# FFN2's seven products in another order, and three small moves around them, in a one-core mLSTM + FFN kernel

## The chip, the core and the metric

The kernel runs on one core of a Trainium2 chip. The core has engines with a queue each, which run side by side and meet only through semaphores: PE (TensorE, matrix products, with PEld for its weight loads), DVE (VectorE), ACT (ScalarE), POOL (GpSimd) and SP (SyncE, which here only issues DMAs). PE writes its products into PSUM, eight banks per partition; DVE and ACT read them from there. The metric is the time of one execution in microseconds (us) on the device; lower is better.

## The reference

An mLSTM cell over 4 batches, 8 heads, 768 steps and 40 features per head, and behind it a feed-forward network with a squared ReLU. The cell's output, 3072 rows of 320 features, is the network's input.

```python
for t in range(S):                       # per batch and head
    m_new = maximum(f[t] + m, i[t])
    fs, is_ = exp(f[t] + m - m_new), exp(i[t] - m_new); m = m_new
    C = fs * C + is_ * outer(v[t], k[t]);  n = fs * n + is_ * k[t]
    y[t] = sigmoid(o[t]) * (C @ q[t]) / maximum(abs(n @ q[t]), 1)
x = y.transpose(0, 2, 1, 3).reshape(3072, 320)
h = maximum(x @ w_in, 0)                 # 320 -> 2048
out = (h * h) @ w_out                    # 2048 -> 320
```

The FFN weights come as 8-byte floats, which the kernel rounds early on; these products are fp32.

## The kernel before

**Tiling.** The sequence is cut into 24 blocks of 128 tokens (`s` = 0..23, six for each batch), and the FFN into 12 groups of two blocks, 256 tokens (`g` = 0..11). Attention of block `s` is computed chunk-wise: scores, weighted values, a carried state C, and the numerators, which DVE turns (`tn`, L858) and SP stores to DRAM (`store_num`, L873) and loads back token by token (`load_num`, L878). `normalise_turned` (L883 to L903, DVE) then makes the FFN's input rows x, which go through DRAM once more (`store_rows` L931, `load_rows` L936) and are turned by DVE into `xT` (L943).

**FFN2 as seven products.** The second FFN product of groups 1 to 11 (`ffn2_fast`, L1066) takes the 256 tokens x 2048 hidden x 320 outputs as 2 x 2 blocks and needs seven block products in place of eight. Call the blocks of the hidden values A11, A12, A21, A22 (first index: token half; second: even or odd hidden blocks) and those of w_out B11 to B22. Sums of weight blocks (T0, T1, T2, and B12 overwritten by a difference) are made once. Sums of the A blocks are made by DVE for each group in `sums` (L1044 to L1056), 128 x 1024 elements each: S1 = A21 + A22, S2 = S1 - A11, then "S3" = A11 - A21, which overwrites A21, and S4 = A12 - S2. A product (`product`, L1058 to L1061) is 8 fp32 matmuls of 128 x 160 that accumulate in one bank; the trace records 16 instructions for it.

The seven products, in PE's order, with the bank and the reader of each:

| | product | bank | read by |
|---|---|---|---|
| 1 | A11 B11 | X | ACT copies it to m1 (L1081) |
| 2 | S2 T1 | Y | DVE: u12 = Y + m1 (L1077) |
| 3 | A12 B21 | on top of X | ACT copies it to the output y0 (L1086) |
| 4 | S3 B12 | on top of Y | DVE: m1 += Y |
| 5 | S1 T0 | X' | DVE: u22 = m1 + X' |
| 6 | A22 T2 | Y' | DVE: m1 += Y' |
| 7 | S4 B22 | on top of X' | DVE: u12 += X' |

All five DVE additions have the line L1077. `ffn2_fast` is called in four steps: step 0 issues products 1 and 2, step 1 products 3 and 4, step 2 products 5 and 6, step 3 product 7.

**The order of the work.** The kernel runs under a manual schedule: each engine executes its instructions in the order in which the program issues them, and the tile layer adds the semaphore waits (a reader waits for the writer, and a writer of a bank or tile waits for the last reader of what it overwrites). The main loop (L1440 on) walks through `parts`: for each `g` four steps of FFN2 of group `g` and four parts of FFN1 of group `g + 2` (`ffn1_open` L1145, `ffn1_close` L1178, `ffn1_rows` L1161). Each run of four parts carries one attention block: even `s` goes with FFN2, odd `s` with FFN1. A block for which `joined(s)` holds (even, 10 or later) has its first half of attention inside the FFN1 part before. Five PSUM banks (`ps_h`) serve FFN1, FFN2 and half of the scores; three (`ps_at`) the rest of attention. A new `ps_h` tile gets the bank that has been out of use longest.

**The places the change touches** are, besides `ffn2_fast`: S2 of the coming group, issued after `ffn1_close` (L1544) and so ahead of `attend_end`'s turns of the numerators (L858) and sums for the state C (L865, L869) in DVE's queue; S3 and S4 of group 1 at loop steps `n` = 8 and 9 (L1513, L1515); SP's order, in which `load_rows` of an odd block (L1453) stands ahead of `store_num` of the even block after it (L1490), and `load_A` (L430, the gate rows for a block two later) ahead of `load_num`.

Of the kernel before, what the change touches and what calls it, by code (L numbers as in the profile page):

```python
# [9 lines left out]
F32 = mybir.dt.float32  # L10
# [7 lines left out]
P = 128  # L18
# [11 lines left out]
def kernel(  # L30
# [27 lines left out]
    nc = tc.nc  # L58
    B, H, S, D = q.shape
    BH = B * H  # L60
    NB = S // P
# [7 lines left out]
    NPAIR = NF // 2  # L69
    GT = 2  # L70
    NG = NT // GT
    W = 4 * P
# [12 lines left out]
    ps_h = banks.enter_context(tc.tile_pool(name="ps_h", bufs=3, space=PSUM))  # L85
# [234 lines left out]
    st = {}  # L320
# [83 lines left out]
    def turn_kq(s):  # L404
        t = kqT_b[s % NKT][:].rearrange("p n j t -> p (n j t)")
        nc.vector.transpose(t, t)
# [522 lines left out]
    def store_rows(s):  # L929
        t = st[s]["xT"] = xT_half(s).rearrange("p c t -> p (c t)")  # L930
        nc.sync.dma_start(x_d[s].rearrange("c t d -> t c d"), st[s]["x"][:].rearrange("p (c d) -> p c d", c=3))  # L931

    def load_rows(s):
        t = st[s]["xT"]
        for r in range(P // SQ):
            nc.sync.dma_start(  # L936
                t[r * SQ : (r + 1) * SQ].rearrange("p (b a) -> p b a", a=SQ),
                x_d[s, :, :, r * SQ : (r + 1) * SQ].rearrange("c (n p) a -> p (c n) a", p=SQ),
            )
# [85 lines left out]
    DH = DM // 2  # L1025
    wo = w_out[:].rearrange("p (f two) d -> p f two d", two=2)
    B11, B12 = wo[:, :, 0, :DH], wo[:, :, 0, DH:]
    B21, B22 = wo[:, :, 1, :DH], wo[:, :, 1, DH:]
    T = {}
# [14 lines left out]
    def sums(g, ps, which=(1, 2, 3, 4)):  # L1044

        if "S" not in st:
            st["S"] = [late.tile([P, NPAIR, P], F32, name=f"S{n}", bufs=1) for n in (1, 2, 4)]
        S1, S2, S4 = (t[:, ps] for t in st["S"])
        g4 = st["g2", g][:].rearrange("p (f two) t -> p f two t", two=2)[:, ps]
        A11, A12, A21, A22 = (g4[:, :, i, n * P : (n + 1) * P] for n in range(2) for i in range(2))  # L1050
        for n in which:
            to, a, b, op = {
                1: (S1, A21, A22, ALU.add), 2: (S2, S1, A11, ALU.subtract),
                3: (A21, A11, A21, ALU.subtract), 4: (S4, A12, S2, ALU.subtract),
            }[n]
            nc.vector.tensor_tensor(to, a, b, op=op)  # L1056

    def product(to, lhsT, rhs, start=False):  # L1058

        for p in range(NPAIR):  # L1060
            nc.tensor.matmul(  # L1061
                to, lhsT=lhsT[:, p], rhs=rhs[:, p, :], start=(start and p == 0), stop=(p == NPAIR - 1),
                skip_group_check=True,
            )

    def ffn2_fast(g, step):  # L1066

        if step == 0:
            st["y"] = [ffn.tile([P, DM], F32, name="y_sb", bufs=3) for _ in range(2)]
        if step in (0, 2):  # L1070
            st["o2"] = [ps_h.tile([P, W], F32, name="h_ps") for _ in range(2)]
        (X, Y), (y1, y0) = st["o2"], st["y"]
        g4 = st["g2", g][:].rearrange("p (f two) t -> p f two t", two=2)
        cols = [slice(n * P, (n + 1) * P) for n in range(2)]
        S1, S2, S4 = st["S"]
        X, Y = X[:, :DH], Y[:, :DH]
        add = lambda to, a, b: nc.vector.tensor_tensor(to, a, b, op=ALU.add)  # L1077
        m1, u12, u22 = y1[:, :DH], y0[:, DH:], y1[:, DH:]
        if step == 0:
            product(X, g4[:, :, 0, cols[0]], B11, start=True)  # L1080
            nc.scalar.copy(m1, X)  # L1081
            product(Y, S2, T[1], start=True)
            add(u12, Y, m1)
        elif step == 1:
            product(X, g4[:, :, 1, cols[0]], B21)
            nc.scalar.copy(y0[:, :DH], X)  # L1086
            product(Y, g4[:, :, 0, cols[1]], B12)
            add(m1, m1, Y)
            if g + 1 == NG:
                nc.sync.dma_start(out[g * GT * P : (g * GT + 1) * P, :DH], y0[:, :DH])  # L1090
        elif step == 2:
            product(X, S1, T[0], start=True)
            add(u22, m1, X)
            if g + 1 < NG:
                sums(g + 1, slice(0, NPAIR), (1,))
            product(Y, g4[:, :, 1, cols[1]], T[2], start=True)
            add(m1, m1, Y)
            t = g * GT + 1
            nc.sync.dma_start(out[t * P : (t + 1) * P, :], y1[:])
        else:  # L1100
            product(X, S4, B22)
            add(u12, u12, X)
            t = g * GT
            to = slice(DH if g + 1 == NG else 0, DM)
            nc.sync.dma_start(out[t * P : (t + 1) * P, to], y0[:, to])
# [107 lines left out]
    def do(f, s):  # L1213
        if 0 <= s < NT:
            f(s)
# [97 lines left out]
    for u in range(8):  # L1313
        s = 2 + u // 2
# [107 lines left out]
    ps_h = ctx.enter_context(tc.tile_pool(name="ps_h", bufs=5, space=PSUM))  # L1422
# [14 lines left out]
    def joined(s):  # L1437
        return EARLY <= s < NT and s % 2 == 0

    for n, (which, g, i) in enumerate(parts):  # L1440
        s, at = NB + n // 4, n % 4
# [7 lines left out]
            half_tanh(7)  # L1449
        if at == 3 and not even and s + 3 > EARLY:  # L1450
            do(load_squares, s + 3)
            if joined(s + 1):
                load_rows(s)  # L1453
        if at == 0 and even and s < EARLY:
            do(scores, s)
            do(weighted, s)
# [8 lines left out]
        if at == (0 if joined(s) else 1):  # L1465
            if not joined(s):
                do(attend_begin, s)
            if s + 1 == EARLY:
                turn_kq(EARLY)
            if n == 5:  # L1470
                sums_of_weights(3)
            if even:
                do(lambda s: scores(s, ("h" if s < EARLY else False, "h")), s + 1)
            if fast:
                ffn1_rows(g, 0, True)
                if joined(s + 1):
                    scores(s + 1, (False, "h"))
            do(attend_end, s)
            do(decays, s + 1)
            if not even and s > EARLY + 1:  # L1480
                do(half_tanh, s)
            do(mask, s + 1)
            if not even and not fast:
                do(turn_kq, s + 1)
            do(decay_C, s + 1)
            if not fast and not even:
                do(turn_squares, s - 1)
            if s == NB + 2:
                load(s + 3)
            do(store_num, s)  # L1490
            if s > NB + 1:
                do(load_A, s + 2)
            if n == 1:
                normalise_turned(5)
                store_rows(5)
                turn_squares(4)
            if n == 5:
                load_rows(6)
            do(load_num, s)
            if n == 1:  # L1500
                load_rows(5)
                weigh(7, masked=True)
                sums_of_win(2)
            if s + 2 <= EARLY:
                do(load_squares, s + 2)
            if even and s <= NB + 1:
                do(load_A, s + 2)
        if n == 3:
            load_o(8)
            load_o(9)  # L1510
            sums_of_weights(0)
        if n == 8:
            sums(1, slice(0, NPAIR), (3,))  # L1513
        if n == 9:
            sums(1, slice(0, NPAIR), (4,))  # L1515
            sums_of_weights(2)
            turn_squares(6)
# [19 lines left out]
        if fast:  # L1537
            if i % 2:
                if n == 7:
                    sums(1, slice(0, NPAIR), (2,))  # L1540
                early = (lambda: attend_begin(s + 1)) if at == 3 and joined(s + 1) else None
                ffn1_close(g, i // 2, i == 1, early)
                if early:
                    sums(g - 1, slice(0, NPAIR), (2,))  # L1544
                if at == 1:
                    if s + 1 < EARLY:
                        do(turn_kq, s + 1)
                    if n > 5:
                        do(turn_squares, s - 1)
            else:  # L1550
                if at == 2 and joined(s + 1):
                    weigh(s + 1, masked=True)
                    weighted(s + 1)
                ffn1_open(g, i // 2)
                if at == 2 and joined(s + 1):
                    do(scale_q, s + 1)
                    do(turn_kq, s + 2)
                    normalise_turned(s)
                    store_rows(s)
                    do(load_o, s + 5)  # L1560
                if i == 0 and g > 2 and not joined(s + 1):
                    sums(g - 1, slice(0, NPAIR), (2,))
            if at == 2 and not joined(s + 1):
                do(scale_q, s + 1)
            if n == 6:
                sums(1, slice(0, NPAIR), (1,))
        elif g == 0:
            ffn2(i)
        else:
            ffn2_fast(g, i)  # L1570
# [80 lines left out]
```

## Time and profile before

| | |
|---|---|
| time, median of 3 runs | 488.17 us (486.13 to 489.63) |
| the profiled execution | 486.8 us, span of its instructions 485.1 us |
| PE busy | 473.7 us, 98% of the span |
| DVE, ACT, POOL busy | 343.4, 243.4, 225.3 us |
| granted TensorE clock | 1.00 |

The span is the time from the first to the last instruction of the program; the rest of the execution lies outside it. A busy share says how much of the span an engine had work in flight; since matmuls overlap each other, the starts of PE's rows tell more than their lengths. In a row of the timeline the first column is the start, the second the length, and a number in square brackets is the idle time of the engine just ahead of it, with what ended it.

### The profile page before, as it was taken

Reading aid. Unit: us, or ns where it says so; the run is one execution under the profiler, and the core shown is the slowest. Engines: PE = TensorE matmul, PEld = TensorE weight load, DVE = VectorE, ACT = ScalarE, POOL = GpSimd, SP = SyncE. Lnnn points to the kernel's source line nnn. Section 1 sums busy time; section 2 is a strip of 40 time slices with the busy share of each in tenths; the row PEclk is TensorE's granted clock in tenths of the full one; section 3 lists DMA queues with packets and bytes.
Section 4 is the critical chain, followed back from the end, with each engine's and each line's share of the span. In section 5 each row is a group of like instructions: output and inputs, shape, how many; then the busy total and the mean of one; then the engine's idle time right before and its main releaser. Section 6 shows DMA issues by size and latency. Waiting matters only on the chain.

```text
span 485.1 us, 15702 instructions
## 1 busy us (share of the span) xinstructions
PE 473.7 (98%) x6387; PEld 442.2 (91%) x6389; DVE 343.4 (71%) x725; ACT 243.4 (50%) x534; POOL 225.3 (46%) x337
## 2 busy tenths in 40 slices
PE   8989999999999999998999999999999999999997
PEld 4876788779899999898999999999999999999997
DVE  7969868788886955864965966965965957635441
ACT  4699897644744543543653652553553551513300
POOL 4464545567881955825836826824923111020000
PEclk9999999999999999999999999999999999999999
DMA  8999997779996798676687676896773312200000
GB/s 167 204 271 257 275 219 189 208 147 232 204 189 149 168 156 187 137 146 151 151 146 165 152 148 149 163 151 138 146 143 86 93 54 82 55 22 9 1 28 27
DMA packets 192839, 69.93 MB, mean 144 GB/s; under 512 B 158144, under 2 KB 181504, under 8 KB 192768
## 3 DMA queue, kind: packets, MB, share of 16 engines
q1 hardware_dynamic: 157424, 56.39, 52.1%
q0 software_dynamic: 6080, 10.16, 9.5%
q10 hardware_dynamic: 29264, 2.39, 4.7%
q8 instruction: 50, 0.82, 0.8%
q14 instruction: 21, 0.17, 0.1%
HBM read 55.69 MB, written 18.92 MB: 154 GB/s over the span
## 4 chain that ended last, share of the span: by engine, by line
PE 57%; DVE 0%; issue 0%
PE h_ps L1061 28%; PE h_ps L1140 18%; PE h_ps L1173 5%; PE numT L823 2%; PE numT L801 1%; PE tp L587 1%; PE numT L835 1%; DVE S L1056 0%; PE h_ps L587 0%; DVE g L1195 0%; DVE y_sb L1077 0%
## 5 line engine op out<-in xcount | busy, mean ns | idle before, releaser
L1061 PE MATMUL h_ps<-T,S 128*128 128x160 f32 x352 | 51.6, 299 | 0.9 <-DVE S L1056 0.9
L1061 PEld LDWEIGHTS h_ps<-T,S 128*128 128x128 f32 x352 | 48.9, 190 | 1.1 <-PE h_ps L1061 1.1
L1061 PE MATMUL h_ps<-w_out,g 128*128 128x160 f32 x336 | 48.8, 301 | 0.0
L1061 PEld LDWEIGHTS h_ps<-w_out,g 128*128 128x128 f32 x336 | 46.2, 190 | 1.1 <-issue 0.5
L1077 DVE TENSOR_TENSOR y_sb<-y_sb,h_ps 128x160 f32<-128x160 f32 x44 | 14.0, 318 | 44.7 <-PE h_ps L1061 44.7
L1154 ACT COPY r_sb<-h_ps 128x512 f32<-128x512 f32 x20 | 11.7, 585 | 65.8 <-PE h_ps L1140 40.8
L1140 PE MATMUL h_ps<-xT,w_in 128*128 128x128 f32 x320 | 43.3, 278 | 0.0
L1140 PE MATMUL h_ps<-lent_t,w_in 128*128 128x128 f32 x320 | 42.3, 275 | 0.0
L1132 POOL TENSOR_TENSOR lent_t<-xT 128x128 f32<-128x128 f32 (+1 forms) x18 | 10.3, 591 | 66.6 <-DVE xT L943 54.1
L1140 PEld LDWEIGHTS h_ps<-xT,w_in 128*128 128x128 f32 x320 | 39.2, 192 | 1.6 <-issue 1.2
L375 POOL DMA_DIRECT2D va<-in_v_dram x64 | 39.5, 634 | 0.2 <-issue 0.2
L1173 PE MATMUL h_ps<-xT,w_in 64*64 64x128 f32 x960 | 39.3, 272 | 0.0
L1140 PE MATMUL h_ps<-lent_t 128*128 128x128 f32 x320 | 39.1, 275 | 0.0
L1140 PEld LDWEIGHTS h_ps<-lent_t,w_in 128*128 128x128 f32 x320 | 38.9, 192 | 0.0
L1140 PEld LDWEIGHTS h_ps<-lent_t 128*128 128x128 f32 x320 | 37.3, 192 | 0.2 <-issue 0.2
L510 ACT ACTIVATE A_bc<-A_bc,b_R 128x64 f32<-128x64 f32 (+1 forms) x128 | 35.6, 363 | 0.1
L1173 PEld LDWEIGHTS h_ps<-xT,w_in 64*64 64x64 f32 x960 | 35.1, 133 | 0.6
L1191 ACT ACTIVATE g<-h_ps 128x512 f32<-128x512 f32 x12 | 7.2, 597 | 52.0 <-PE h_ps L1140 34.8
L479 POOL TENSOR_SCALAR_AFFINE_SELECT A_bc<-A_bc 64x512 f32<-64x512 f32 x32 | 25.6, 800 | 16.0 <-ACT kq L497 14.8
L858 DVE STREAM_TRANSPOSE tn<-numT 128x256 f32<-128x256 f32 x36 | 13.9, 424 | 24.4 <-PE numT L801 16.8
L977 PE MATMUL h_ps<-xT,w_in 128*128 128x256 f32 x128 | 29.9, 386 | 0.4 <-POOL w_in L236 0.4
L531 POOL TENSOR_TENSOR vw<-va,A_bc 128x328 f32<-128x328 f32 x13 | 11.5, 886 | 39.8 <-ACT A_bc L510 39.8
(231 smaller groups left out, 1209.4 us busy)
## 6 DMA issues: line engine op xcount, KB each, us to landing
A_bc<-a_slots SPq DMA_DIRECT2D x32, 256.0 KB, 4.3
kq<-num_rows SPq DMA_DIRECT2D x80, 64.0 KB, 3.5
num_rows<-tn SPq DMA_DIRECT2D x18, 256.0 KB, 2.4
raw<-in_moe_w_out_dram SPq DMA_DIRECT2D x7, 640.0 KB, 5.1
og<-in_o_gate_dram SPq DMA_DIRECT2D x24, 160.0 KB, 5.0
x_rows<-x_sb SPq DMA_DIRECT2D x20, 192.0 KB, 2.7
xT<-x_rows SPq DMA_DIRECT2D x80, 48.0 KB, 2.9
out_dram<-y_sb SPq DMA_DIRECT2D x23, 160.0 KB, 2.6
```

The lines of the kernel that those rows point to most:

```text
L375: eng.dma_start(dst[HALVES[n], PR * (1 - late_keys) : PR * (2 - late_keys)], src[HALVES[late_keys], PR * m : PR * (m + 1)],)
L479: nc.gpsimd.affine_select(part, part, compare_op=ALU.is_ge, fill=-1e30, base=0, pattern=[[0, PR], [0, 2], [1, DP]], channel_multiplier=-1,)
L510: nc.scalar.activation(A[0][:, x, to], A[0][:, x, to], AF.Exp, bias=b_R[:, b, c, own, x : x + 1],)
L531: nc.gpsimd.tensor_tensor(d["vw"][:].rearrange("p (own x) d -> p own x d", own=2), d["va"][:].rearrange("p (own x) d -> p own x d", own=2) ...
L858: nc.vector.transpose(to[:, 2 * m : 2 * m + 2], d["numT"][m].rearrange("p c t -> p (c t)"))
L977: nc.tensor.matmul(hs[i][:, n, :], lhsT=w_in[:, a, fb * P : (fb + 1) * P], rhs=xT[:, :, a, :], start=(n == 0 and a == 0), stop=False,)
L1061: nc.tensor.matmul(to, lhsT=lhsT[:, p], rhs=rhs[:, p, :], start=(start and p == 0), stop=(p == NPAIR - 1), skip_group_check=True,)
L1077: add = lambda to, a, b: nc.vector.tensor_tensor(to, a, b, op=ALU.add)
L1132: sub = lambda to, a, b: eng.tensor_tensor(to, a, b, op=ALU.subtract)
L1140: nc.tensor.matmul(to[:, n, :], lhsT=lhsT[:, 4 * q + n, :], rhs=rhs, start=(start and n == 0), stop=True, skip_group_check=True,)
L1154: nc.scalar.copy(m1[:], X[:])
L1173: nc.tensor.matmul(to[cols, n, :], lhsT=w_in2[rows, 4 * q + n, cols], rhs=rhs, start=(start and n == 0), stop=True, skip_group_check=True,)
```

## The change

- The products are issued as A11 B11, **S1 T0**, A12 B21, **S2 T1**, S3 B12, A22 T2, S4 B22. S1 T0 goes second, into a bank V that stays open until the seventh product is added on top of it. S2 T1 goes fourth, into a bank Y, and S3 B12 is added on top of Y right behind it. The addition u12 = Y + m1, which reads Y between the two, moves from behind the second product to behind the fourth; u22 = m1 + V stays behind the fifth.
- S2 of a group is issued behind `attend_end`, so behind DVE's turns of the numerators and its sums for C. S3 of group 1 moves from `n` = 8 to `n` = 9.
- For the joined blocks SP issues `store_num` first, then `load_rows` of the block before, then `load_num`, then `load_A`.

```diff
-        if step in (0, 2):
-            st["o2"] = [ps_h.tile([P, W], F32, name="h_ps") for _ in range(2)]
-        (X, Y), (y1, y0) = st["o2"], st["y"]
+        o2 = st.setdefault("o2", {})
+        for name in ("XV", "Y", "Z", "")[step]:
+            o2[name] = ps_h.tile([P, W], F32, name="h_ps")[:, :DH]
+        y1, y0 = st["y"]
...
         if step == 0:
-            product(X, g4[:, :, 0, cols[0]], B11, start=True)
-            nc.scalar.copy(m1, X)
-            product(Y, S2, T[1], start=True)
-            add(u12, Y, m1)
+            product(o2["X"], g4[:, :, 0, cols[0]], B11, start=True)
+            nc.scalar.copy(m1, o2["X"])
+            product(o2["V"], S1, T[0], start=True)
         elif step == 1:
-            product(X, g4[:, :, 1, cols[0]], B21)
-            nc.scalar.copy(y0[:, :DH], X)
-            product(Y, g4[:, :, 0, cols[1]], B12)
-            add(m1, m1, Y)
+            product(o2["X"], g4[:, :, 1, cols[0]], B21)
+            nc.scalar.copy(y0[:, :DH], o2["X"])
+            product(o2["Y"], S2, T[1], start=True)
+            add(u12, o2["Y"], m1)
...
         elif step == 2:
-            product(X, S1, T[0], start=True)
-            add(u22, m1, X)
+            product(o2["Y"], g4[:, :, 0, cols[1]], B12)
+            add(m1, m1, o2["Y"])
+            add(u22, m1, o2["V"])
             if g + 1 < NG:
                 sums(g + 1, slice(0, NPAIR), (1,))
-            product(Y, g4[:, :, 1, cols[1]], T[2], start=True)
-            add(m1, m1, Y)
+            product(o2["Z"], g4[:, :, 1, cols[1]], T[2], start=True)
+            add(m1, m1, o2["Z"])
...
         else:
-            product(X, S4, B22)
-            add(u12, u12, X)
+            product(o2["V"], S4, B22)
+            add(u12, u12, o2["V"])
...
-            if joined(s + 1):
-                load_rows(s)
...
             do(attend_end, s)
+            if joined(s):
+                sums(s // 2 - 3, slice(0, NPAIR), (2,))
             do(decays, s + 1)
...
             do(store_num, s)
-            if s > NB + 1:
+            if joined(s):
+                load_rows(s - 1)
+            elif s > NB + 1:
                 do(load_A, s + 2)
...
             do(load_num, s)
+            if joined(s):
+                do(load_A, s + 2)
...
-        if n == 8:
+        if n == 9:
             sums(1, slice(0, NPAIR), (3,))
-        if n == 9:
             sums(1, slice(0, NPAIR), (4,))
...
                 ffn1_close(g, i // 2, i == 1, early)
-                if early:
-                    sums(g - 1, slice(0, NPAIR), (2,))
```

More of the change, by code (lines that the diff above doesn't have):

```diff
@@ L1075, in ffn2_fast @@
         S1, S2, S4 = st["S"]
-        X, Y = X[:, :DH], Y[:, :DH]
         add = lambda to, a, b: nc.vector.tensor_tensor(to, a, b, op=ALU.add)
```

## The prediction

> **What bounds the kernel now.** The page comes first: which engine is full, and whether it waits.
>
> ```profile
> PE 473.7 (98%) x6387; PEld 442.2 (91%) x6389; DVE 343.4 (71%) x725; ACT 243.4 (50%) x534; POOL 225.3 (46%) x337
> ...
> PE 57%; DVE 0%; issue 0%
> ...
> L1061 PE MATMUL h_ps<-T,S 128*128 128x160 f32 x352 | 51.6, 299 | 0.9 <-DVE S L1056 0.9
> ...
> L1077 DVE TENSOR_TENSOR y_sb<-y_sb,h_ps 128x160 f32<-128x160 f32 x44 | 14.0, 318 | 44.7 <-PE h_ps L1061 44.7
> ```
>
> PE is busy 98% of the span and carries the chain that ended last. DVE's additions wait for PE (44.7 us in all), not the other way round. So whatever makes PE wait is added to the time, and the most that can be saved is what PE waits now. That is in the waits of PE alone:
>
> ```profile
> PE numT L835 <- issue: 1.4, 1, 1.4
> ...
> PE h_ps L1061 <- DVE S L1056: 0.9, 1, 0.9
> ...
> PE numT L835 <- DVE kq L792: 0.5, 1, 0.5
> PE h_ps L587 <- DVE kqT L406: 0.5, 1, 0.5
> ```
>
> From FFN2's groups on, these four are all there is. S2 holds PE up in one group of eleven, 0.9 us.
>
> Then I read FFN2 itself in the timeline, PE's rows and DVE's, group 5:
>
> ```profile
> 282.01 4.51 PE L1061 MATMUL h_ps<-w_out,g_c 128*128 128x160 f32 x32
> 286.35 2.34 PE L1061 MATMUL h_ps<-T,S 128*128 128x160 f32 x16
> 288.53 2.34 PE L1061 MATMUL h_ps<-T,g_c 128*128 128x160 f32 x16
> 290.70 2.34 PE L1061 MATMUL h_ps<-w_out,S 128*128 128x160 f32 x16
> ```
> ```profile
> 286.55 0.32 DVE L1077 TENSOR_TENSOR y_sb<-y_sb,h_ps 128x160 f32<-128x160 f32 x1 [1.42 <-PE h_ps L1061]
> ...
> 288.73 0.32 DVE L1077 TENSOR_TENSOR y_sb<-y_sb,h_ps 128x160 f32<-128x160 f32 x1 [1.25 <-PE h_ps L1061]
> ...
> 290.90 0.32 DVE L1077 TENSOR_TENSOR y_sb<-y_sb,h_ps 128x160 f32<-128x160 f32 x1 [0.72 <-PE h_ps L1061]
> ```
>
> PE starts a product every 2.17 us, without a gap. DVE takes up a finished product 0.20 us after PE has begun the next one (286.35 to 286.55, and so at 288.53 and 290.70), and its addition takes 0.32 us. Today nobody waits for that: between two products into the same bank there is always a third, 2.17 us long, which covers 0.20 + 0.32.
>
> **The new wait.** In the new order S2 T1 and S3 B12 go into bank Y one right behind the other, and u12 must read S2 T1 alone in between. In the built program the first matmul of the fifth product waits for the DVE addition u12 of its group, in all eleven groups. So PE stands from the end of the fourth product's issue until that addition is done. Behind it on PE stand products 5 to 7 and the next FFN1 part: all that is left.
>
> *Price of one hand-over.* 0.20 until DVE begins, 0.32 for the addition, then PE's restart behind a DVE result. Three rows show restarts: L406 ends at 131.59 and PE starts at 131.64 (0.05); L792 133.12 and 133.17 (0.05); S2 205.22 and 205.37 (0.15). The product behind the last takes 2.25 us (205.37 to 207.62) where the others of that place take 2.19 (279.82 to 282.01): 0.06 for filling up again. Together 0.63 to 0.73; I take the middle, 0.68. Nothing hides it.
>
> [...]
>
> *Groups 3 to 11:* DVE is free in time. What stands ahead of u12 in its queue is S2, S3, S4 and the turn L406, and L406 ends 0.9 to 1.7 us before product 4 does (211.19 and 212.16, 249.24 and 250.17, 285.13 and 286.55, 321.27 and 322.43, 357.14 and 358.82; groups 8 to 11 have no L406 there). 9 x 0.68 = **6.1**.
>
> *Group 2:* L406 waits for a load and ends at 175.59, so u12 takes 175.51 to 175.84; product 5 would start at 174.99 and starts at 175.94 with a restart of 0.10. With refilling **1.0**.
>
> *Group 1:* here the change first gains. The addition u12 and S3 (132.62, 131.52) no longer stand ahead of L792, which frees PE: the wait of 0.53 at 133.17 goes, some 0.68 in starts. But DVE now runs S3 behind the turns (the rows of before 0.68 earlier, and S3's 1.1 put in): 133.43 turns, 134.42 S3, 135.52 S4, 136.64 T2, 138.32 the turn of xT, 138.88 u12, done at 139.2. Product 5 starts at 139.3 in place of 138.44: with refilling a net loss of **0.9**.
>
> **What goes.** S2 is due as fourth product instead of second. Its wait in group 3 (product 2 starts 3.29 us after product 1, in other groups 2.28) goes: **-1.1** with the refilling. What is late next there is L1193, which frees the bank of the second product: done at 202.74, product 2 due at 204.36. In all other groups S2 was in time already; moving it saves nothing there.
>
> **What moves at no cost.** S2 waits for three DVE pieces more, some 1.0 us (0.77 and 0.35, overlapping): done near 280.6 in group 5, due at 284.2. S3 and S4 shift by less than DVE's free time. u22 now follows another addition: 0.5 us later, and product 7, which needs it, has product 6 between. C and the turned numerators come 1.5 us earlier; POOL (Cd, L768) and DVE's later x rows gain, and PE waits for neither. On SP, store, loads of x, load of the numerators and the gate rows change places. The x loads move back by one issue, 0.4 us (in group 8, where SP reaches the store before DVE is done, 1.5), and the transposes L943 that need them today start over 2 us after they land; the gate rows come 2 to 4 us later, and the mask that reads them stands an attention block on. Without that cover a late x would hold up FFN1, at the length of the delay. The copies, the banks of FFN1 and the tail behind the last product stay: V is free again only at the end of product 7, but the next to take that bank is the scores tile, five tiles on, as X' was.
>
> **Sum:** 6.1 + 1.0 + 0.9 - 1.1 = **+6.9 us**; with restarts of 0.05 or 0.15 throughout, 6.4 to 7.5. On the profiled execution that is 486.8 + 6.9 = 493.7; it is 1.4 under the median of the runs, so on the median 488.2 + 6.9 = **495.1 us**, 1.4% slower. About 1% is what a measurement of this kernel can tell from no change.
>
> **Rivals.**
> - *The hand-over costs PE next to nothing (not slower).* Place: the first matmul of product 5. If PE could start it while DVE reads, the price is 0 and what remains are the gains, 1.1 + 0.7: 486.4. The result would be no slower once a hand-over costs under 0.16 (1.8 / 11). For it: no row of before shows this very wait. Against: restarts elsewhere always come behind DVE's end. 5%.
> - *DVE comes late to u12 in more groups.* L406 hangs on loads of kq rows, which had DVE idle for 0.4 to 1.6 us; SP's new order moves them. If they come 2 us later in groups 3 to 7, u12 follows by about 1 in each: 500. Against: those loads are issued ahead of the part of SP's queue that changes. 10%.
> - *The clock drops.* [...] Against: behind the stands of 0.85 and 1.4 us the rate is full (2.25 a product). [...] 2%.
> - *The change does more than it says:* the lone "issue" wait of 1.4 us, which no engine explains, falls elsewhere or not at all: 493.7. 10%.
>
> The forecast has 73%. **Range** 491.8 to 498.5: below, the low sum 6.4 without the issue wait on the profiled execution (486.8 + 6.4 - 1.4); above, the high sum on the slowest run (489.6 + 7.5 = 497.1) and part of the way to the late DVE. **Chances**: slower by over 1% (over 493.05) 0.85; within 1% 0.14; faster 0.01.
>
> **What would show it.** L1061 among PE's waits on DVE y_sb L1077, eleven times, 0.4 to 1.0 us each, 6 to 8 us in all; no wait on S L1056; product 5 starting 2.8 to 2.9 us after product 4; L792's wait gone. Wrong if that wait is shorter than 0.2, or if another new wait of PE stands beside it.

## The result, and the profile after

| | before | after |
|---|---|---|
| median of 6 runs each | 487.3 us (484.95 to 489.63) | 493.4 us (492.47 to 495.59) |
| span of the profiled execution | 485.1 us | 491.3 us |
| granted TensorE clock | 1.00 | 1.00 |

The ratio of after to before is 1.0138, with a 95% interval of 1.0101 to 1.0175: the change makes the kernel 1.4% slower, 6 to 7 us. The engines' busy times and the costliest groups, on the page of the kernel after:

```profile
PE 475.2 (97%) x6387; PEld 442.0 (90%) x6389; DVE 342.9 (70%) x725; ACT 243.5 (50%) x534; POOL 224.1 (46%) x337
...
L1061 PE MATMUL h_ps<-w_out,g 128*128 128x160 f32 x336 | 50.6, 304 | 4.6 <-DVE y_sb L1077 4.6
...
L1061 PE MATMUL h_ps<-T,S 128*128 128x160 f32 x352 | 51.4, 299 | 0.0
...
L1077 DVE TENSOR_TENSOR y_sb<-y_sb,h_ps 128x160 f32<-128x160 f32 x44 | 14.1, 320 | 32.0 <-PE h_ps L1061 31.7
...
L1061 PE MATMUL h_ps<-w_out,g_c 128*128 128x160 f32 x192 | 28.8, 303 | 3.2 <-DVE y_sb L1077 3.2
```

No engine has much more or less work than before; PE's 473.7 us of busy time have become 475.2, which is little more than eleven refills behind a wait at 0.11 (1.2; worked out below). What differs is the idle time in front of the groups: the products with S (second row) have lost their 0.9, and the products with the weights themselves, among them S3 B12, wait for the additions of DVE, 4.6 and 3.2 us. In the waits of PE, all of it is one entry:

```profile
PE h_ps L1061 <- DVE y_sb L1077: 7.7, 11, 1.7
...
PE numT L823 <- issue: 0.6, 2, 0.3
...
PE h_ps L587 <- DVE kqT L406: 0.4, 1, 0.4
```

The columns are microseconds in total, how often, and the longest. Eleven waits in eleven groups, as forecast; the waits on S2 (L1056), on L792 and the single "issue" wait of 1.4 us are not there any more. Two small "issue" waits have come, 0.3 each, at 314.72 and 375.92. Two of the eleven waits, those of groups 1 and 2, last 1.7, above the 0.4 to 1.0 that the prediction named. The timeline of PE, of DVE and of the weight loads (PEld) in group 5 shows one hand-over:

```profile
284.74 2.34 PE L1061 MATMUL h_ps<-T,S 128*128 128x160 f32 x16
287.55 2.44 PE L1061 MATMUL h_ps<-w_out,g_c 128*128 128x160 f32 x16 [0.47 <-DVE y_sb L1077]
289.83 2.34 PE L1061 MATMUL h_ps<-T,g_c 128*128 128x160 f32 x16
292.00 2.34 PE L1061 MATMUL h_ps<-w_out,S 128*128 128x160 f32 x16
```
```profile
287.17 0.33 DVE L1077 TENSOR_TENSOR y_sb<-h_ps,y_sb 128x160 f32<-128x160 f32 x1 [1.01 <-PE h_ps L1061]
```
```profile
287.55 1.52 PEld L1061 LDWEIGHTS h_ps<-w_out,g_c 128*128 128x128 f32 x11 [0.71 <-DVE y_sb L1077]
```

Product 4 starts at 284.74 and would be followed at 286.91. DVE had been idle for 1.01 us and begins u12 at 287.17, when the product is through PE; the addition ends at 287.50, and product 5 starts at 287.55. The idle time in the bracket, 0.47, is not the price: from start to start it is 2.81 in place of 2.17, and the next interval is 2.28 in place of 2.17, so a hand-over costs 0.64 + 0.11 = **0.75 us**. All nine groups from 3 to 11 show the same to 0.02.

Where the 6.2 us of the two spans come from, by the start of each group's first product (after less before; the last is the end of the last product):

| group | 1 | 2 | 3 | 4 | 5 | 6 | 7 | 8 | 9 | 10 | 11 | end |
|---|---|---|---|---|---|---|---|---|---|---|---|---|
| difference, us | -0.81 | +0.16 | +1.76 | -0.14 | +0.58 | +1.53 | +2.28 | +3.16 | +3.92 | +4.67 | +5.42 | +6.16 |

It goes up by about 0.75 a group (0.95 and 0.88 where the two "issue" waits lie, from group 5 to 6 and from 7 to 8), by 1.0 and 1.6 across groups 1 and 2, and falls once, by 1.9 from group 3 to group 4: there the S2 wait (1.09 in starts) and the "issue" wait of before, about 1.5 in starts, are missing, less one hand-over. The -0.81 ahead of the first group lies in a stretch before FFN2. Group 2 itself costs 2.0, as worked out further down; 0.4 of it comes back because the stretch from its end to group 3 takes 20.00 us in place of 20.41.

### The profile page after: what moved, and what is told of

The parts are those of the page before. It is cut to its first block, busy times and chain, and to the rows that moved or that the text cites. A ratio compares the mean times of both kernels' runs of the same rounds, so it can differ in the third digit from the quotient of the medians.

```text
span 491.3 us, 15677 instructions
## 1 busy us (share of the span) xinstructions
PE 475.2 (97%) x6387; PEld 442.0 (90%) x6389; DVE 342.9 (70%) x725; ACT 243.5 (50%) x534; POOL 224.1 (46%) x337
## 4 chain that ended last, share of the span: by engine, by line
PE 83%; DVE 4%; ACT 4%; DMA 4%; issue 2%; POOL 2%; SPq 1%; DVEq 0%; POOLq 0%
PE h_ps L1061 31%; PE h_ps L1140 24%; PE h_ps L1173 7%; PE h_ps L977 4%; PE h_ps L1015 4%; PE numT L823 3%; PE numT L801 2%; PE tp L587 2%; PE numT L835 1%; DMA og<-in_o_gate_dram 1%; DMA kqT<-kq_rows 1%; PE h_ps L988 1%; PE tp L595 1%; ACT g_c L516 1%; DVE y_sb L1077 1%
## 5 line engine op out<-in xcount | busy, mean ns | idle before, releaser
L1061 PE MATMUL h_ps<-w_out,g 128*128 128x160 f32 x336 | 50.6, 304 | 4.6 <-DVE y_sb L1077 4.6
L1132 POOL TENSOR_TENSOR lent_t<-xT 128x128 f32<-128x128 f32 (+1 forms) x18 | 11.4, 652 | 76.1 <-DVE xT L943 47.8
L1077 DVE TENSOR_TENSOR y_sb<-y_sb,h_ps 128x160 f32<-128x160 f32 x44 | 14.1, 320 | 32.0 <-PE h_ps L1061 31.7
L1061 PE MATMUL h_ps<-w_out,g_c 128*128 128x160 f32 x192 | 28.8, 303 | 3.2 <-DVE y_sb L1077 3.2
L1061 PEld LDWEIGHTS h_ps<-w_out,g_c 128*128 128x128 f32 x192 | 26.5, 190 | 4.7 <-DVE y_sb L1077 4.1
```

The lines of the kernel that those rows point to most:

```text
L1061: nc.tensor.matmul(to, lhsT=lhsT[:, p], rhs=rhs[:, p, :], start=(start and p == 0), stop=(p == NPAIR - 1), skip_group_check=True,)
```

## The experiments

The theory: the whole loss is the hand-over in bank Y; the order of SP's queue and the place of S2 on DVE cost PE nothing in the changed kernel. Rivals: the new order on SP delays the kq tiles and so u12; the late S2 costs something; the wait only shows a lateness that lies elsewhere. Each of the seven kernels was timed against runs of the kernel before on the same chip, and ratios are to those runs.

### A bank of its own for the fifth product

```diff
-            product(o2["Y"], g4[:, :, 0, cols[1]], B12)
-            add(m1, m1, o2["Y"])
+            product(o2["X"], g4[:, :, 0, cols[1]], B12, start=True)
+            add(m1, u12, o2["X"])
```

> The changed kernel with its fifth product (S3 B12) started afresh in bank X, which the first and third product have left by then, so that nothing accumulates behind the read of bank Y; the add behind it becomes m1 = u12 + X, so VectorE has as many adds as before. Theory (the whole loss is the hand-over in bank Y): TensorE's 11 waits on the add of u12, 7.7 us of idle time, and their refills, 0.1 each, go; the profiled span falls from 491.3 to about 482.5, the median from 493.4 to about 484.5 to 486, a little faster than the kernel before (487.3), since the wait on S2 in group 3 and the one on the numerators' transposes in group 1 stay away. Rival (the order of SP's queue, or the late kq tiles, cost part of it): groups 1 and 2 stay longer than before by about 1 each and the median is 487 to 489. Rival (the hand-over is only the place where another lateness shows): the wait turns up at another product or at FFN1's first one, and the median stays above 491.

Measured: 483.1 us against 484.9 for the kernel before, ratio **0.9976 (0.9952 to 0.9999)**; span 481.6. As a share of its kernel before, the theory's range is 0.994 to 0.997, and the first rival's begins at 0.999. Two of PE's waits that are left (the first lies early, at 33.86 us), and PE's and DVE's rows in group 5:

```profile
PE tp L555 <- DMA kq<-in_q_dram: 0.7, 1, 0.7
PE h_ps L1061 <- DVE y_sb L1077: 0.4, 1, 0.4
```
```profile
281.02 2.34 PE L1061 MATMUL h_ps<-T,S 128*128 128x160 f32 x16
283.19 2.34 PE L1061 MATMUL h_ps<-w_out,g_c 128*128 128x160 f32 x16
285.36 2.34 PE L1061 MATMUL h_ps<-T,g_c 128*128 128x160 f32 x16
```
```profile
283.45 0.33 DVE L1077 TENSOR_TENSOR y_sb<-h_ps,y_sb 128x160 f32<-128x160 f32 x1 [2.03 <-PE h_ps L1061]
```

Product 5 follows product 4 after 2.17 us again (281.02 to 283.19), with DVE doing u12 in the same place, at 283.45, beside it. One wait of 0.4 on L1077 is left, at the sixth product of group 1, where DVE is late. Against the changed kernel this is 1.0138 / 0.9976 = 1.016, some 8 us (by the two intervals, give or take 2), for an edit that removes nothing but the second use of bank Y. So the loss is the hand-over, and the rest of the change does not cost anything that can be measured. The kernel lies 0.2% below the kernel before, with an interval that just leaves out no difference; two kernels further down (0.9977 and 0.9989) cannot be told from it.

### The new order of products alone

The kernel before with the new `ffn2_fast`; S2, S3, S4 and SP's queue stay as they were.

```diff
-            product(Y, S2, T[1], start=True)
-            add(u12, Y, m1)
+            product(o2["V"], S1, T[0], start=True)
...
+            product(o2["Y"], S2, T[1], start=True)
+            add(u12, o2["Y"], m1)
...
+            product(o2["Y"], g4[:, :, 0, cols[1]], B12)
```

> The kernel before with the new order of FFN2's products alone; the places of S2, S3 and S4 on VectorE and the order of SP's queue are those of before. Theory: 9 hand-overs of 0.75 in groups 3 to 11 (6.8), 1 to 1.8 each in groups 1 and 2 where VectorE comes to the add late, less the wait on S2 in group 3 (1.1) and the one in group 1 (0.5 to 0.7): about 6 to 8 above the kernel before, 493.5 to 495.5 at a median of 487.3 for it. Rival (S2's place and SP's order cost it): within 2 of the kernel before.

Measured: 1.0159 (1.0106 to 1.0212), +7.7 us; span 490.4. PE's wait:

```profile
PE h_ps L1061 <- DVE y_sb L1077: 7.1, 11, 2.2
```

As the theory had it: this edit makes the loss by itself, with the S2 wait and the L792 wait gone too. In groups 3 to 11 the two intervals are 2.81 and 2.28 as in the changed kernel.

### The new order of SP's queue alone

```diff
-            if joined(s + 1):
-                load_rows(s)
...
             do(store_num, s)
-            if s > NB + 1:
+            if joined(s):
+                load_rows(s - 1)
+            elif s > NB + 1:
                 do(load_A, s + 2)
...
             do(load_num, s)
+            if joined(s):
+                do(load_A, s + 2)
```

> The kernel before with the new order of SP's queue alone: the store of the even numerators ahead of the x loads, the gate rows behind the reload. Theory (TensorE sees none of it): within 0.7 of the kernel before. Rival (the kq tiles of the next chunk land later behind it, as in group 2 of the changed kernel, 1.2 us later than before): VectorE's transpose of kq in group 2 starts 1 us later than before, and with no hand-over to delay it still costs TensorE little, up to 1 us. If it costs more than 1.5, the forecast's zero for SP's order is wrong.

Measured: 0.9989 (0.9960 to 1.0017). It costs nothing that can be measured; the interval goes from 1.9 us less to 0.8 us more. This run and the others also bear on whether SP's order delays group 2. There DVE's turn L406, which stands ahead of u12, began 9.19 us after the group's first product in the changed kernel and 8.15 us in the kernel before, and I had suspected the new order of SP. Over all executions the same distance is 8.15, 9.65, 8.66 and 8.85 with the old order of SP and 9.19, 8.95, 7.89, 7.86 and 9.38 with the new one. It varies by 1.8 us from one execution to the next, and not with the order, as far as these nine show. The rows of DVE in group 2 of the changed kernel show what u12 hangs on:

```profile
175.54 1.25 DVE L406 STREAM_TRANSPOSE kqT<-kqT 128x1024 f32<-128x1024 f32 x1 [4.33 <-DMA kqT<-kq_rows]
176.71 0.28 DVE L1077 TENSOR_TENSOR y_sb<-h_ps,y_sb 128x160 f32<-128x160 f32 x1
```

The wait on S2 moves between executions, too: this kernel has S2 where the kernel before has it, and waits for it in groups 2 and 4 (0.7 in all) and not in group 3.

### The addition u12 twice

```diff
             add(u12, o2["Y"], m1)
+            add(u12, o2["Y"], m1)
```

> The changed kernel with the add of u12 issued twice, which writes the same values. Theory (the fifth product waits for the end of VectorE's last read of bank Y): each of the 11 waits grows by one add, 0.32, so 3.5 in all, or up to 4.4 if the second add does not follow the first at once (0.4 each): 496.9 to 497.8 at a median of 493.4 for the changed kernel. Rival (the restart of TensorE is set by something other than the add): within 1 of the changed kernel.

Measured: 1.0223 (1.0185 to 1.0262), that is 0.84% or 4.1 us more than the changed kernel, between the 3.5 and the 4.4 expected. The two intervals leave room for 1.5 to 6.7, so the rows say more than the times. PE's waits and group 5:

```profile
PE h_ps L1061 <- DVE y_sb L1077: 10.6, 11, 2.3
```
```profile
284.21 2.34 PE L1061 MATMUL h_ps<-T,S 128*128 128x160 f32 x16
287.38 2.44 PE L1061 MATMUL h_ps<-w_out,g_c 128*128 128x160 f32 x16 [0.83 <-DVE y_sb L1077]
```
```profile
286.65 0.68 DVE L1077 TENSOR_TENSOR y_sb<-h_ps,y_sb 128x160 f32<-128x160 f32 x2 [1.64 <-PE h_ps L1061]
```

The interval is 3.17 in place of 2.81: one more addition, 0.36 us, appears in full on PE, and so in all nine groups from 3 to 11 (3.2 us). The waits in all grow by 2.9, since DVE came earlier in group 2 of this execution. Product 5 starts 0.05 behind the end of the second addition (287.33, 287.38), as it started 0.05 behind the only one.

### The new order with a bank of its own, S2 and SP as before

The bank of its own from the first experiment, put into the kernel of the second one (the new order alone). The expectation's "second kernel of this study" is that of the first experiment, the changed kernel being the first.

```diff
-            product(o2["Y"], g4[:, :, 0, cols[1]], B12)
-            add(m1, m1, o2["Y"])
+            product(o2["X"], g4[:, :, 0, cols[1]], B12, start=True)
+            add(m1, u12, o2["X"])
```

> The kernel before with the new order of products and the fifth product in bank X as in the second kernel of this study (own_bank), while S2 stays early on VectorE and SP's queue keeps its old order. Theory (the hand-over was all of the loss, and S2's place and SP's order are worth nothing by themselves): within 0.4% of own_bank, so 0.994 to 1.001 of the kernel before, some 9 us under order_only by its span (490.4 - 7.1 of waits - 1 of refills = 482). Rival (the late S2 or the new order of SP is what made own_bank the faster one): 2 or more slower than own_bank.

Measured: 0.9977 (0.9945 to 1.0009), the same as with S2 late and SP in the new order (0.9976), each known to about 0.3%. So the two together are worth nothing that can be measured once S2 T1 is the fourth product. No wait on L1077 is left in its list.

### Another product between the two of bank Y

```diff
+            add(u22, m1, o2["V"])
...
+            product(o2["Z"], g4[:, :, 1, cols[1]], T[2], start=True)
             product(o2["Y"], g4[:, :, 0, cols[1]], B12)
-            add(m1, m1, o2["Y"])
-            add(u22, m1, o2["V"])
...
-            product(o2["Z"], g4[:, :, 1, cols[1]], T[2], start=True)
+            add(u22, u22, o2["Y"])
             add(m1, m1, o2["Z"])
+            add(m1, m1, o2["Y"])
```

> The changed kernel with the product in bank Z (T2) put between the two that share bank Y: order X, V, X, Y, Z, Y, V. u22 = m1 + V is formed early and takes bank Y in an add of its own, so VectorE has one add more in each group (0.32). Theory (a read between two products of one bank costs nothing while another bank's product of 2.2 runs beside it: 0.20 + 0.32 is far below that, except where VectorE comes late by more than 2): the 11 waits go as with a bank of its own, 0.994 to 1.001 of the kernel before. Rival (TensorE waits at the other product of bank Y all the same, or VectorE's further add delays group 1 or 2): 1.003 to 1.01.

Measured: 1.0021 (0.9993 to 1.0049), just above the range of the theory and below that of the rival, with an interval that reaches into both. PE's waits say why:

```profile
PE h_ps L1061 <- DVE T L1039: 1.5, 1, 1.5
```

No wait on L1077 is left: the eleven hand-overs are gone, without any further bank, because the product in Z runs beside DVE's read of Y (282.63, 284.80, 286.98: 2.17 each in group 5). But A22 T2 now comes one place earlier, and in group 1 its weights T2, which DVE makes just then, are late by 1.5, where the kernel with its own bank waits 0.4 at the same product. That accounts for 1.1 of the 2.2 us (0.45%) between these two kernels; the rest is within the two intervals and stays open.

### S2 late, in the old order of products

The kernel before with S2 behind `attend_end`, and with S3 of group 1 at `n` = 9, as in the changed kernel; products and SP as they were.

```diff
-                if early:
-                    sums(g - 1, slice(0, NPAIR), (2,))
...
             do(attend_end, s)
+            if joined(s):
+                sums(s // 2 - 3, slice(0, NPAIR), (2,))
...
-        if n == 8:
+        if n == 9:
             sums(1, slice(0, NPAIR), (3,))
-        if n == 9:
             sums(1, slice(0, NPAIR), (4,))
```

> The kernel before with S2 behind the numerators' transposes on VectorE, as in the changed kernel, but FFN2's products and SP's queue in the old order, so that S2 T1 is still the second product. Theory (the two edits belong together: in the changed kernel S2 was done 2.8 after the start of group 5's first product, while the second product starts 2.28 after it and could follow 0.05 to 0.1 behind S2): a wait of about 0.6 in each of groups 2 to 8 in place of those of the kernel before, 3 to 6 above the kernel before. Rival (VectorE is ahead of TensorE without the other edits, too): within 1.5 of it.

Measured: 1.0079 (1.0045 to 1.0112), +3.8 us. PE's waits, and group 4:

```profile
PE h_ps L1061 <- DVE S L1056: 5.9, 6, 1.7
```
```profile
239.44 2.44 PE L1061 MATMUL h_ps<-w_out,g 128*128 128x160 f32 x16
243.23 2.41 PE L1061 MATMUL h_ps<-T,S 128*128 128x160 f32 x16 [1.34 <-DVE S L1056]
```

The mechanism and the total are those expected, the single wait is longer (1.0 on average, in groups 2 to 7) and comes less often. So the edits are not independent: a late S2 costs 3.8 while S2 T1 is the second product and nothing that can be measured once it is the fourth. By the ratios, the parts alone are +7.7, +3.8 and -0.5, and together +6.7.

## Why the prediction was right

- **The new wait** is in all eleven groups, at the first matmul of product 5, on u12, and nothing else of weight appeared beside it. That it is the cause and not the place is shown by three kernels: with a bank of its own it goes and so does the loss; with a product in between it goes, and 1.0138 becomes 1.0021; with one addition more it grows by that addition.
- **Its price** was put at 0.68 and is 0.75. Waiting for DVE to begin (0.20 of the old rows) and the addition (0.33) were right to 0.07 together: 287.17 less 286.91 is 0.26 and not 0.20. Restart was 0.05, the low end. The refilling was mis-sized: 0.11 and not 0.06; 0.02 of that is the row it was compared with, which took 2.19 where undisturbed ones take 2.17. Nine groups give 6.75 in place of 6.1. The weight load of product 5 starts at 287.55, together with its matmul, and its own row says that it waited for the same addition ([0.71 <-DVE y_sb L1077]).
- **Group 2** is the term with the largest error: 1.0 predicted, 2.0 measured (the interval was 4.08, and 2.28 behind it). The working took L406's time from one execution, and that time hangs on a load that moves by 1.8 us from one execution to the next; in that of the changed kernel it came 1.04 later, which is the whole error. The runs do not show what moves it, only that SP's order has no visible part in it.
- **Group 1**, +0.9 net predicted: the start of product 5 lies 14.09 behind that of product 1 in place of 13.22, and with the refilling the loss is 0.98. The L792 wait is gone as worked out.
- **The S2 wait** in group 3: -1.1 predicted, -1.09 measured. That is the size in one execution of the kernel before; in the kernel with SP's new order, S2 was waited for 0.7, in other groups.
- **The moves at no cost** cost nothing that can be measured: SP's order by itself is 0.9989 of before, and S2's place and SP's order together are worth 0.0001 between the two kernels with their own bank. For S2 the cover named, its due place as fourth product, is needed: without it, 3.8 us.
- **The lone "issue" wait** of 1.4, the fourth rival, did fall away. Six of the other traces have no "issue" wait in FFN2's stretch. The kernel of the fifth experiment has one of 0.9 at the same place: in L835, behind 7.1 us of the work that follows group 3, as before. Both kernels have SP's old order, but so have two of the six. So it looks like a matter of the single execution and not of the change, but nine traces do not prove it, and what PE waits for there stays open. A profile of before without it would have been 1.4 shorter.
- **The sum**, +6.9, was 6.2 on the spans and 6.1 on the medians, and it was so by terms that offset each other: +0.65 in nine groups, +1.0 in group 2, +0.1 in group 1 and +0.3 for the two new "issue" waits more than predicted; -1.5 for the old "issue" wait, -0.4 between groups 2 and 3, and -0.8 ahead of FFN2, whose start lies anywhere from 124.1 to 126.7 us in the nine traces. That the total came out nearer than its terms is luck. Of the 1.7 us between the 495.1 forecast and the 493.4 measured, 0.9 is the kernel before: 487.3 over six runs in place of 488.2 over three.
- Of the rivals, "next to nothing" falls by the 0.75 of every group. "DVE late in more groups" falls too: in groups 3 to 11 DVE waited for PE before u12. The clock stayed at 1.00 in the profiled execution of the changed kernel.

## What to carry to other kernels

In this kernel two products that accumulate in one PSUM bank, with a read by another engine between them, cost PE that read in full when they stood back to back: 0.75 us each time, for a read of 0.33. Put the second into a bank that is free by then and add it on the other engine, or put a product of another bank between them, which here ran for 2.17; both removed all eleven waits. Look then at what the product that moved needs: A22 T2, one place earlier, waited 1.5 for its weights. When two edits are made together, ask of each what it would cost alone: here the one (S2 late) needed the other (S2 T1 fourth), and the other cost more than it brought.

## What was unexpected

In the kernel with the new order alone, group 2 had the longest stand of PE (a stretch in which it does nothing), 2.20 us, and behind it the granted clock fell. The windows of that trace (start and end, length, busy time of PE, PEld, DVE, ACT and POOL, granted clock, DMA share, GB/s), and PE's rows:

```profile
175.57:176.50 0.93, 0.93 (x7) 0.93 (x8) 0.54 (x1) 0.00 (x0) 0.00 (x0) 1.00 0.75 238
176.50:177.50 1.00, 1.00 (x7) 1.00 (x6) 0.00 (x0) 0.00 (x0) 0.00 (x0) 0.60 0.93 225
177.50:178.50 1.00, 1.00 (x6) 1.00 (x5) 0.00 (x0) 0.00 (x0) 0.00 (x0) 0.50 1.15 216
178.50:179.50 1.00, 1.00 (x6) 1.00 (x5) 0.32 (x1) 0.00 (x0) 0.00 (x0) 0.50 1.42 187
179.50:180.50 1.00, 1.00 (x7) 1.00 (x7) 0.97 (x3) 0.00 (x0) 0.00 (x0) 0.69 1.30 157
```
```profile
175.57 3.58 PE L1061 MATMUL h_ps<-w_out,g_c 128*128 128x160 f32 x16 [2.20 <-DVE y_sb L1077]
178.94 2.92 PE L1061 MATMUL h_ps<-T,g_c 128*128 128x160 f32 x16
181.69 2.34 PE L1061 MATMUL h_ps<-w_out,S 128*128 128x160 f32 x16
```

PE restarts at a granted clock of 1.00, and about 1.1 us later the clock is halved for some 3.4 us (0.8 of the second window at 0.50, two whole ones, 0.6 of the last). The products take 3.37 and 2.75 in place of 2.28 and 2.17, so the stand cost 1.67 us more than its length. A stand of 2.28 us in group 1 of the kernel with u12 twice had no such sequel (clock 1.00, next product 2.28), nor had that of 1.74 in group 2 of the changed kernel. A drop also came without a single stand of that length. The kernel with a bank of its own and the one that adds this bank to the new order alone each have a lower mean granted clock in one stretch of 20 us, long before group 1: 0.91 from 40 to 60 us and from 20 to 40 us, and 1.00 in every other stretch. (By estimate it is a drop of the same size: 3.4 us at 0.50 would give a mean of 0.915 over 20 us.) In the lists of PE's waits of these two kernels the longest single wait is 1.0 and 1.5 us. What brings the drop on, and why stands of about equal length differ, these runs do not show. For the hand-over itself the clock played no part in the profiled execution: none of the changed kernel's eleven stands, 0.47 to 1.74 us, had such a sequel (granted clock 1.00). Three of its six executions have a mean granted clock of 0.993 to 0.997, as some of the kernel before have; where in them it fell is not on record.
